# Leaving out the product of mean and inverse root in one batch's normalisation

## The chip, the cores and the metric

The kernel runs on one core of a Trainium2 chip. The core has five engines with a queue each: TensorE (PE, matmuls), VectorE (DVE), ScalarE (ACT), GpSimd (POOL) and SyncE (SP, which issues most DMAs). The metric is the device time of one execution in microseconds, as the median of several runs.

## The reference, cut to what matters

A windowed attention with sink columns feeds a gated MLP block. The change lies in the layer normalisation of the MLP's second half, `v`.

```python
x = attention(q, k, v, n_sink, window)          # 4 batches, 768 rows, 512 columns
h = gelu_tanh(x @ w_in)                         # 1024 columns
u, v = h[..., :512], h[..., 512:]
mu = mean(v, -1); var = mean((v - mu) ** 2, -1)
v_n = (v - mu) / sqrt(var + 1e-6) * g_ln
v_s = einsum('ts,bsd->btd', w_sg, v_n) + b_sg[None, :, None]
out = x + (u * v_s) @ w_out
```

## The kernel before, in words

Attention is done for 16 pairs of heads (numbers 0 to 15, four to a batch). The MLP block follows once for each of the four batches b = 0 to 3 and is woven into the attention of the next pairs. A batch's 768 rows are six tiles j = 0 to 5 of 128 rows.

Every step of the program is an operation with a name, such as `hv13` (batch 1, tile 3). The string `FIRST` lists all names in the order in which they are written out, and the string `TAKERS` says which engine takes a step that could go to several. `Planner.run` walks through `FIRST`; each engine gets its instructions in that order and runs them in order. Waits between engines are semaphores. So the order on each engine is written out by hand, and an operation that is removed moves nothing but what stands behind it on its own engine.

The steps of one batch that the prediction speaks of are these:

- `hv` b j: PE makes the tile's 512 columns of v (L751). `gelu_v` (ACT, L762) writes them to `v_all`.
- `bn` b j: DVE takes statistics and aggregates them (L773, L774). Mean and variance go to columns 0 and 1 of `mv`, a tile with three numbers for each of the six row tiles.
- `rstd` b 0 and `rstd` b 3: POOL adds 1e-6 to three variances (L818) and raises them to the power -0.5 (L820), for tiles 0 to 2 and for tiles 3 to 5.
- `shift` b 0 and `shift` b 3: DVE writes minus mean times inverse root to column 2 of `mv` (L826).
- `vn` b j: the normalised tile, in bfloat16. On DVE it is (v - mean) times inverse root in one instruction (L840), which reads columns 0 and 1. On ACT it is scale times v plus bias (L836), and the bias is column 2.
- `sp` b f m a and b: PE multiplies vn by the transposed `w_sg` (L864), tiles 0 to 2 in part a and tiles 3 to 5 in part b. `gate` and `gT` (DVE) follow, then `pj` (PE, the output projection).

`TAKERS` gives all six vn of batch 1 to DVE; batches 0, 2 and 3 give some of theirs to ACT. The vn of batch 1 stand in `FIRST` as vn10 vn11 vn12, then vn15, vn14, vn13. Around them POOL casts the pairs' rows to bfloat16 (L249: `cast_k`, `cast_q`, `cast_v`).

Of the kernel before, what the change touches and what calls it, by code (L numbers as in the profile page):

```python
# [49 lines left out]
class Planner:  # L50
# [15 lines left out]
    def add(self, *args, **kwargs):  # L66
        op = Op(*args, **kwargs)
        self.ops.append(op)
        return op
# [86 lines left out]
    "peek_DVE copied look"  # L156
)
TAKERS = (
    "zero_a0:ACT zero_a1:DVE zero_a2:DVE zero_a3:DVE low_a:DVE zero_b0:DVE zero_b1:DVE "
# [19 lines left out]
def kernel(  # L179
# [49 lines left out]
        vn=([128, NT, DF], BF16), gT=([128, KU, S], BF16), gv=([128, NH], BF16),  # L229
        o_sb=([128, DM], F32), st=([128, 6], F32))  # L230

    def tile_of(tag):
        shape, dtype = shapes[tag]
        return work.tile(shape, dtype, name=tag, tag=tag, bufs=R[tag].size)
# [6 lines left out]
    T = {}  # L241
    add = plan.add
# [10 lines left out]
    WARM = 8  # L253
    AHEAD = (0, 1)
    LAST = (2, 3)
    MARK = (B - 1, 3)
    LONG = ()
    BY_DMA = (11,12,13,14,15)
# [76 lines left out]
    def make_mask(m, at):  # L335
        for h in range(2):
# [6 lines left out]
                    rank=-2000)  # L343
    T["dark0"] = add("dark0", {"DVE": 450}, lambda _: make_dark0(), [T["dark"]], use=[dark],
                     rank=-1998)
    T["mask"] = add("mask", {"DVE": 600}, lambda _: make_mask(mask, 1), [T["dark"]],
                    use=[dark], rank=-300)
    T["mask0"] = add("mask0", {"DVE": 600}, lambda _: make_mask(mask0, 0), [T["dark0"]],
                     use=[dark], rank=-299)

    if LONG:
        T["spread"] = add("spread", {"POOL": 900}, lambda _: make_spread(), new=[spread],
                          rank=-378)
# [83 lines left out]
    def pos(n):  # L437
        return divmod(n, HP)
# [371 lines left out]
    def normalise(b, js, rank):  # L810
        mv = T["mv", b]
        lo, hi = js[0], js[-1] + 1
        if lo == 0:
            T["vn", b] = Buf(R["vn"])
        vn, v_all = T["vn", b], T["v_all", b]

        def root(_):
            nc.gpsimd.tensor_scalar(out=mv.tile[:, lo:hi, 1:2], in0=mv.tile[:, lo:hi, 1:2],  # L818
                                    scalar1=1e-6, scalar2=None, op0=ALU.add)
            nc.gpsimd.tensor_tensor(out=mv.tile[:, lo:hi, 1], in0=mv.tile[:, lo:hi, 1],  # L820
                                    in1=half[:, lo:hi], op=ALU.pow)

        r = add(f"rstd{b}{lo}", {"POOL": 1250}, root, [T["bn", b, j] for j in js], use=[mv],
                rank=rank)
        def shift(_):
            nc.vector.scalar_tensor_tensor(  # L826
                out=mv.tile[:, lo:hi, 2], in0=mv.tile[:, lo:hi, 0], scalar=-1.0,
                in1=mv.tile[:, lo:hi, 1], op0=ALU.mult, op1=ALU.mult)

        r = add(f"shift{b}{lo}", {"DVE": 160}, shift, [r], use=[mv], rank=rank)  # L830
        for j in js:
            def norm(e, j=j):
                if j == 0:
                    vn.tile = tile_of("vn")
                if e == "ACT":
                    nc.scalar.activation(out=vn.tile[:, j, :], in_=v_all.tile[:, j, :],  # L836
                                         func=AF.Identity, scale=mv.tile[:, j, 1:2],
                                         bias=mv.tile[:, j, 2:3])
                else:
                    nc.vector.tensor_scalar(  # L840
                        out=vn.tile[:, j, :], in0=v_all.tile[:, j, :],
                        scalar1=mv.tile[:, j, 0:1], scalar2=mv.tile[:, j, 1:2],
                        op0=ALU.subtract, op1=ALU.mult)
            T["vnorm", b, j] = add(
                f"vn{b}{j}", {"DVE": 700, "ACT": 800}, norm, [r] + ([T["vnorm", b, 0]] if j else []),
                new=[vn] if j == 0 else [], use=[v_all, mv] + ([vn] if j else []),
                rank=rank + 1)

# [41 lines left out]
    def project(b, t, rank, rooms):  # L890
# [3 lines left out]

        halves = [slice(0, DM)] if (b, t) != LAST else \
            [slice(0, DM // 2), slice(DM // 2, DM)]
# [115 lines left out]
    def turn_g(_):  # L1012
# [5 lines left out]
            rank=9000)  # L1018
# [39 lines left out]
    for n in range(NP):  # L1058
        r = 100 * n
        b, hp = pos(n)  # L1060
# [73 lines left out]

    held_o = T["o_sb", *MARK]

# [18 lines left out]
    for e in EARLY:  # L1155
        add("peek" if e == "SP" else f"peek_{e}", {e: 100 if e == "DVE" else 750}, peek, [a], rank=0)
    T["st", -1, 0] = add("copied", {"DVE": 150}, copied, [a, T["st", *MARK]], use=[held_o],
                         rank=0)
# [183 lines left out]
```

## Time and profile before

| | |
|---|---|
| median of 3 runs | 161.76 us (161.67 to 161.82) |
| the profiled execution's own time | 163.07 us |
| its span, first to last instruction | 161.1 us |
| mean granted clock of PE | 0.996 |
| instructions | 4001 |
| from HBM, to HBM | 24.81 MB, 6.29 MB |

The table says that the profile was taken of an execution 1.31 us above the median, with 1.94 us outside its span. A row of a timeline gives start, duration, engine, line, operation, the tiles written and read, their shapes and a count; in brackets stands how long the engine was idle before it, and what ended that.

### The profile page before, as it was taken

How to read it: one execution, taken by the hardware profiler on the slowest of the kernel's cores; microseconds unless marked ns; L12 is line 12 of the kernel's file. 1: busy time of each engine (PE TensorE's matmuls, PEld its weight loads, DVE VectorE, ACT ScalarE, POOL GpSimd, SP SyncE). 2: the span in 40 equal slices, each digit the busy share in tenths (PEclk: the TensorE clock that was granted, in tenths of full speed). 3: DMA queues.
4: the chain of work that ended last, by engine and by line, in shares of the span. 5: the costliest groups of instructions: out<-in, count | busy, mean ns of one | idle time of the engine just before them, and what ended most of it. 6: DMA issues, size and time to landing. Idle time of an engine off the chain costs nothing. (4 is left out here: it accounts for less than half of the span.)

```text
span 161.1 us, 4001 instructions
## 1 busy us (share of the span) xinstructions
PE 150.1 (93%) x1547; PEld 87.3 (54%) x1562; DVE 130.5 (81%) x283; ACT 107.5 (67%) x143; POOL 83.6 (52%) x126
## 2 busy tenths in 40 slices
PE   6789999998899999999989999999999999999980
PEld 2335665566656766546556555555556645555540
DVE  7555678695898989969999979868999969888980
ACT  6168878695989877988857778665997168811100
POOL 3465761228688789067975880865579602300000
PEclk9999999999999999999999999999999999999998
DMA  4999999998999986999988889999993340140163
GB/s 146 299 270 305 205 151 206 168 289 231 358 336 240 342 130 163 241 315 234 215 142 209 209 177 216 206 300 257 241 216 114 90 158 0 50 148 4 65 259 141
DMA packets 67877, 32.42 MB, mean 201 GB/s; under 512 B 56564, under 2 KB 64772, under 8 KB 67856
## 3 DMA queue, kind: packets, MB, share of 16 engines
q1 hardware_dynamic: 65328, 29.26, 69.5%
q0 software_dynamic: 2384, 2.75, 10.8%
q8 instruction: 13, 0.21, 0.6%
q10 hardware_dynamic: 144, 0.13, 0.2%
q14 instruction: 8, 0.07, 0.1%
HBM read 24.81 MB, written 6.29 MB: 193 GB/s over the span
## 5 line engine op out<-in xcount | busy, mean ns | idle before, releaser
L627 ACT ACTIVATE ex<-sc 128x1024 bf16<-128x1024 f32 x48 | 47.4, 1024 | 10.5 <-PE sc L610 10.4
L864 PE MATMUL vs<-wsgT,vn 128*128 128x384 bf16 x192 | 35.5, 326 | 1.6 <-DVE vn L840 1.0
L864 PEld LDWEIGHTS <-vn 128*128 128x128 bf16 x192 | 17.5, 98 | 13.2 <-issue 1.6
L793 PE MATMUL hu<-xT,w_in_sb 128*128 128x384 bf16 x128 | 23.4, 326 | 0.0
L801 ACT ACTIVATE uT<-hu 128x384 bf16<-128x384 f32 x32 | 14.9, 490 | 12.3 <-PE hu L793 12.1
L907 PE MATMUL o_ps<-w_out_sb,gT 128*128 128x512 bf16 (+1 forms) x91 | 22.6, 370 | 0.5
L751 PE MATMUL hv<-w_in_sb,xT 128*128 128x512 bf16 x94 | 22.4, 379 | 0.1
L875 DVE SCALAR_TENSOR_TENSOR vs<-vs,g_sb,b_bc 128x384 f32<-128x384 f32 x32 | 19.5, 619 | 2.6 <-PE vs L864 1.3
L773 DVE BATCH_NORM_STATS2 st<-v_all 128x6 f32<-128x512 f32 x24 | 16.3, 678 | 6.5 <-ACT v_all L762 6.5
L311 POOL TENSOR_SCALAR_AFFINE_SELECT ex<-ex 128x512 bf16<-128x512 bf16 (+1 forms) x23 | 15.4, 670 | 9.7 <-ACT ex L627 9.4
L610 PE MATMUL sc<-qT,kT 64*128 64x256 bf16 (+2 forms) x320 | 18.9, 249 | 0.9 <-ACT qT L247 0.5
L249 POOL CAST cast<-k_f 128x768 bf16<-128x768 f32 x16 | 13.4, 840 | 12.0 <-DMA k_f<-in_k_dram 9.4
L676 PEld LDWEIGHTS <-ex 128*128 128x128 bf16 x480 | 16.8, 97 | 4.0 <-issue 1.4
L695 DVE TENSOR_TENSOR x<-av,rcps 128x384 bf16<-128x384 f32 x32 | 17.5, 552 | 0.9
L883 DVE TENSOR_TENSOR gT<-vs,uT 128x384 bf16<-128x384 f32 x32 | 17.5, 555 | 0.9
L676 PE MATMUL av<-v_sb,ex 128*128 128x65 bf16 x352 | 18.0, 194 | 0.1
L249 POOL CAST cast<-q_f 128x768 bf16<-128x768 f32 x15 | 13.0, 869 | 9.7 <-DMA q_f<-in_q_dram 5.0
L918 DVE TENSOR_TENSOR o_sb<-o_ps,x 128x512 f32<-128x512 f32 (+1 forms) x25 | 16.2, 663 | 1.3 <-PE o_ps L907 1.2
L762 ACT ACTIVATE v_all<-hv 128x512 f32<-128x512 f32 x24 | 13.7, 598 | 5.2 <-PE hv L751 5.0
L793 PEld LDWEIGHTS <-w_in_sb 128*128 128x128 bf16 x128 | 12.3, 98 | 8.7 <-issue 0.2
L249 POOL CAST v_sb<-v_f 128x768 bf16<-128x768 f32 x16 | 13.9, 869 | 3.1 <-DMA v_f<-in_v_dram 3.1
L751 PEld LDWEIGHTS <-xT 128*128 128x128 bf16 x96 | 9.2, 98 | 10.5 <-DVE xT L249 0.6
(71 smaller groups left out, 194.2 us busy)
## 6 DMA issues: line engine op xcount, KB each, us to landing
k_f<-in_k_dram SPq DMA_DIRECT2D x16, 384.0 KB, 5.9
q_f<-in_q_dram SPq DMA_DIRECT2D x16, 384.0 KB, 5.2
v_f<-in_v_dram SPq DMA_DIRECT2D x16, 384.0 KB, 6.3
out_dram<-o_sb SPq DMA_DIRECT2D x23, 256.0 KB, 2.2
wsg<-in_moe_w_sg_dram POOLq DMA_DIRECT2D x2, 576.0 KB, 10.8
w_in_sb<-in_moe_w_in_dram POOLq DMA_DIRECT2D x2, 512.0 KB, 8.0
w_out_sb<-in_moe_w_out_dram POOLq DMA_DIRECT2D x1, 512.0 KB, 8.3
b_bc<-in_moe_b_sg_dram SPq DMA_DIRECT2D x1, 384.0 KB
```

What stands on the lines that cost most here:

```text
L249: eng[e].tensor_copy(dst, src)
L610: nc.tensor.matmul(sc.tile[row:row + keys, h, col:col + m], kT.tile[rows, k0:k0 + keys], qT.tile[rows, q0:q0 + m], start=not by_pe, stop=n ...
L627: nc.scalar.activation(out=ex.tile, in_=sc.tile, func=AF.Exp, scale=scale)
L676: nc.tensor.matmul(av.tile[:, m, h, :], ex.tile[:, h, col:col + 128], val, start=first, stop=(m == HT - 1 and h == 1 and at == len(steps) ...
L695: nc.vector.tensor_mul(x.tile[:, hp, HT * c:HT * (c + 1), :].rearrange("p i (h d) -> p i h d", h=2), av.tile[:, :, :, 0:64], rcp.to_broadc ...
L751: nc.tensor.matmul(ps.tile[:, 0:512], xT.tile[:, c, 128 * j:128 * (j + 1)], w_in_sb[:, c, DF:], start=(c == 0), stop=(c == KD - 1))
L773: nc.vector.bn_stats(out=st.tile, in_=v_all.tile[:, j, :])
L793: nc.tensor.matmul(ps.tile[:, 0:NH], w_in_sb[:, c, 128 * f:128 * (f + 1)], xT.tile[:, c, NH * m:NH * (m + 1)], start=(c == 0), stop=(c == ...
L864: nc.tensor.matmul(ps.tile[:, 0:NH], vn.tile[:, si, 128 * f:128 * (f + 1)], wsgT[:, si, cols], start=(si == 0), stop=(si == NT - 1))
L875: nc.vector.scalar_tensor_tensor(out=ps.tile[:, 0:NH], in0=ps.tile[:, 0:NH], scalar=g_sb[:, f:f + 1], in1=b_bc[:, cols], op0=ALU.mult, op1 ...
L883: nc.vector.tensor_mul(gT.tile[:, f, cols], ps.tile[:, 0:NH], uT.tile[:, f, cols])
L907: nc.tensor.matmul(ps.tile[:, 0:w], gT.tile[:, c, 128 * t:128 * (t + 1)], w_out_sb[:, c, cols], start=(c == 0), stop=(c == KU - 1))
```

## The change

The two operations `shift10` and `shift13` are taken out of `FIRST`, and for batch 1 `normalise` no longer makes them. The vn of these groups then follow `rstd` directly, and only DVE may take them. Column 2 of `mv` stays unwritten in batch 1, and nothing reads it there.

```diff
-    "gelu_u130 hu111 gelu_u101 gelu_u111 hu131 sc90 sc91 shift10 bn14 vn10 vn11 gelu_u131 exp91 "
-    "vn12 load_v11 load_k12 load_q12 rstd13 shift13 vn15 pv80 pv81 vn14 vn13 cast_q10 cast_k11 "
...
+    "gelu_u130 hu111 gelu_u101 gelu_u111 hu131 sc90 sc91 bn14 vn10 vn11 gelu_u131 exp91 vn12 "
+    "load_v11 load_k12 load_q12 rstd13 vn15 pv80 pv81 vn14 vn13 cast_q10 cast_k11 dma_k11 rcp80 "
...
     LAST = (2, 3)
+    NO_SHIFT = {(1, 0), (1, 3)}
     MARK = (B - 1, 3)
...
-        r = add(f"shift{b}{lo}", {"DVE": 160}, shift, [r], use=[mv], rank=rank)
+
+        if (b, lo) not in NO_SHIFT:
+            r = add(f"shift{b}{lo}", {"DVE": 160}, shift, [r], use=[mv], rank=rank)
...
-                f"vn{b}{j}", {"DVE": 700, "ACT": 800}, norm, [r] + ([T["vnorm", b, 0]] if j else []),
+                f"vn{b}{j}", {"DVE": 700} if (b, lo) in NO_SHIFT else {"DVE": 700, "ACT": 800}, norm, [r] + ([T["vnorm", b, 0]] if j else []),
```

On DVE, from the aggregate of `bn15` to the first reciprocal of pair 8 (`rcp80`), stood before:

```order
L774 BN_AGGR mv<-st 128x2 [waits DVE_49]
L826 SCALAR_TENSOR_TENSOR mv<-mv 128x3 [waits Pool_49]
L773 BN_STATS st<-v_all 128x6 [waits Activation_49]
L774 BN_AGGR mv<-st 128x2 [waits DVE_49]
L840 TENSOR_SCALAR vn<-v_all,mv 128x512 x3
L826 SCALAR_TENSOR_TENSOR mv<-mv 128x3 [waits DVE_49,Pool_49]
L840 TENSOR_SCALAR vn<-v_all,mv 128x512 x3
L689 RECIPROCAL rcps<-av 128x6 [waits PE_49]
```

The rows of L826 are `shift10` and `shift13`, the rows of L840 the six vn. In the same place on DVE stands now (line numbers are higher by two from there on):

```order
L774 BN_AGGR mv<-st 128x2 [waits DVE_49]
L773 BN_STATS st<-v_all 128x6 [waits Activation_49]
L774 BN_AGGR mv<-st 128x2 [waits DVE_49]
L842 TENSOR_SCALAR vn<-v_all,mv 128x512 [waits Pool_49]
L842 TENSOR_SCALAR vn<-v_all,mv 128x512 x2
L842 TENSOR_SCALAR vn<-v_all,mv 128x512 [waits Pool_49]
L842 TENSOR_SCALAR vn<-v_all,mv 128x512 [waits DVE_49]
L842 TENSOR_SCALAR vn<-v_all,mv 128x512
L689 RECIPROCAL rcps<-av 128x6 [waits PE_49]
```

Two rows are gone, and `bn14` (the statistics and the aggregate) stands directly behind `bn15`. The waits for POOL that the two products carried are now on `vn10` and `vn15`; the wait for an earlier instruction of DVE itself, which `shift13` carried, is on `vn14`. The rows of PE, ACT, POOL and SP up to the end of the computation are the same in number and order.

More of the change, by code (lines that the diff above doesn't have):

```diff
@@ L122 @@
     "gelu_v14 turn_q9 cols_q9 hu101 turn_k10 cols_k10 hu121 gelu_u121 hu120 gelu_u120 hu130 "
[33 rows of a table removed]
-    "peek_DVE copied look"
[33 rows of a table added]
 )
```

62 rows, old and new, of the table FIRST are left out of this document.

## The prediction

> **What bounds the kernel now.** I read the page's busy shares first, then the table of waits, then the timelines of the engines around the one wait that the table left. TensorE (PE) is busy nearly all the time:
>
> ```profile
> PE 150.1 (93%) x1547; PEld 87.3 (54%) x1562; DVE 130.5 (81%) x283; ACT 107.5 (67%) x143; POOL 83.6 (52%) x126
> ```
>
> The waits of PE in the window from 42 to 153 us, that is from the middle of the first batch's block to the last projections, are one row (waiter, who ended it, total us, times, longest):
>
> ```profile
> PE vs L864 <- DVE vn L840: 1.0, 1, 1.0
> ```
>
> So for 110 us PE runs without a pause except one, and that one is ended by a normalised row (vn) from VectorE. The timeline of PE puts it at 81 us, in the second batch:
>
> ```profile
> 79.61 0.65 PE L864 MATMUL vs<-wsgT,vn 128*128 128x384 bf16 x3
> 81.26 0.66 PE L864 MATMUL vs<-wsgT,vn 128*128 128x384 bf16 x3 [0.99 <-DVE vn L840]
> 81.75 0.50 PE L550 MATMUL cps<-iden,cast 128*128 128x128 bf16 x6
> ```
>
> The first three matmuls of batch 1's spatial product (sp100a) start at 79.61; the next three (sp100b) need rows 3 to 5 of vn and start at 81.26. Three matmuls of this kind take 81.75 - 81.26 = 0.49 us from start to start, so sp100b could have begun at 79.61 + 0.49 = 80.10. PE loses 81.26 - 80.10 = **1.16 us** there. Since PE never waits again before 153 us, what it wins here it can keep.
>
> What made vn late is seen on VectorE (DVE; start, duration):
>
> ```profile
> 74.05 0.18 DVE L774 BATCH_NORM_AGGREGATE mv<-st 128x2 f32<-128x6 f32 x1
> 74.21 0.78 DVE L826 SCALAR_TENSOR_TENSOR mv<-mv 128x3 f32<-128x3 f32 x1
> 74.91 0.68 DVE L773 BATCH_NORM_STATS2 st<-v_all 128x6 f32<-128x512 f32 x1
> 75.62 0.18 DVE L774 BATCH_NORM_AGGREGATE mv<-st 128x2 f32<-128x6 f32 x1
> 75.72 1.43 DVE L840 TENSOR_SCALAR vn<-v_all,mv 128x512 bf16<-128x512 f32 x3
> 77.47 0.77 DVE L826 SCALAR_TENSOR_TENSOR mv<-mv 128x3 f32<-128x3 f32 x1 [0.32 <-POOL mv L820]
> 78.16 3.04 DVE L840 TENSOR_SCALAR vn<-v_all,mv 128x512 bf16<-128x512 f32 x3
> 81.12 0.18 DVE L689 RECIPROCAL rcps<-av 128x6 f32<-128x6 f32 x1
> ```
>
> and beside it on GpSimd (POOL):
>
> ```profile
> 74.15 0.82 POOL L249 CAST v_sb<-v_f 128x768 bf16<-128x768 f32 x1
> 75.89 0.43 POOL L818 TENSOR_SCALAR mv<-mv 128x3 f32<-128x3 f32 x1 [0.93 <-DVE mv L774]
> 76.41 1.03 POOL L820 TENSOR_TENSOR mv<-mv,half 128x3 f32<-128x3 f32 x1
> 77.40 0.82 POOL L249 CAST cast<-q_f 128x768 bf16<-128x768 f32 x1
> 78.17 0.82 POOL L249 CAST cast<-k_f 128x768 bf16<-128x768 f32 x1
> 78.94 1.02 POOL L249 CAST v_sb<-v_f 128x768 bf16<-128x768 f32 x1
> 79.91 1.01 POOL L249 CAST cast<-q_f 128x768 bf16<-128x768 f32 x1
> 81.29 0.65 POOL L311 TENSOR_SCALAR_AFFINE_SELECT ex<-ex 128x512 bf16<-128x512 bf16 x1 [0.37 <-ACT ex L627]
> ```
>
> The two removed instructions are the rows of L826 at 74.21 and 77.47. They work on three numbers per partition, yet take 0.78 and 0.77 us. All eight of their kind (count: min/median/max in ns):
>
> ```profile
> L826 DVE SCALAR_TENSOR_TENSOR mv<-mv x8: 131/461/775, 33.8 to 139.6; 128x3 f32<-128x3 f32 x8
> ```
>
> The two in batch 1 start 0.06 and 0.07 us behind a cast on POOL and end 0.02 us after it (74.99 beside 74.97, 78.24 beside 78.22). So the work is 0.13 us, and the rest is held by the cast. The same is seen on vn: three alone take 1.43 us, three beside casts 3.04, and the casts beside them go from 0.82 to 1.02. There DVE and POOL take turns, one vn and one cast in (81.12 - 78.16) / 3 = 0.99 us.
>
> **The change part by part.** *shift10, at 74.21.* Next on DVE is the last statistics instruction (bn14). Its input is the third row here on ScalarE (ACT):
>
> ```profile
> 73.56 0.60 ACT L762 ACTIVATE v_all<-hv 128x512 f32<-128x512 f32 x1 [0.27 <-PE hv L751]
> ...
> 80.19 1.02 ACT L627 ACTIVATE ex<-sc 128x1024 bf16<-128x1024 f32 x1
> 82.29 0.80 ACT L247 COPY qT<-cps 128x768 bf16<-128x768 bf16 x1 [1.08 <-PE cps L550]
> ```
>
> It is there at 73.56 + 0.60 = 74.16, so bn14 can start at about 74.20 in place of 74.91. Would the cast hold it as it held shift10? A statistics row and a cast that lay over each other earlier:
>
> ```profile
> 70.41 0.66 DVE L773 BATCH_NORM_STATS2 st<-v_all 128x6 f32<-128x512 f32 x1
> ```
>
> ```profile
> 70.88 0.83 POOL L249 CAST cast<-k_f 128x768 bf16<-128x768 f32 x1 [1.34 <-DMA k_f<-in_k_dram]
> ```
>
> Both kept their length, so statistics are not held. The removal is worth 74.91 - 74.20 = 0.71 us. With it move vn10 to vn12 (75.72 to 75.01) and, since POOL's chain for rows 3 to 5 waits for the last statistics (the row at 75.89), that chain too: its power ends at 76.41 + 1.03 - 0.71 = 76.73, and the cast of q that follows starts at 77.40 - 0.71 = 76.69.
>
> *shift13, at 77.47.* Now vn15 waits for the power itself, and may start at 76.73 + 0.03 = 76.76. It lands 0.07 us behind a cast, just as shift13 did, so this wait does not go away: it passes to vn15. What goes is one whole turn. Before, the order at the port was q cast, shift13, k cast, vn15, v cast, vn14, q cast, vn13; now it is q cast, vn15, k cast, vn14, v cast, vn13. Before, the three vn took from 78.17 (start of the first cast beside them) to 81.20; now the first cast beside them starts at 76.69, which gives 76.69 + 3.03 = 79.72, or 76.76 + 3.04 = 79.80 counted from vn15. I take 79.80. vn14 has a wait of its own for an earlier DVE instruction, which shift13 carried before: it costs nothing if that is long done (the statistics are), at most 0.11 us, since an aggregate, which waits for the statistics in front of it, starts 0.03 us after their end (75.59, 75.62) where a row without such a wait starts 0.08 us before it (78.24, 78.16). 79.91 then.
>
> *PE.* sp100b needs vn13 0.06 us ahead (81.20, then 81.26), so by 80.04. Either end meets this with 0.1 us or more to spare, and the gain is PE's whole 1.16 us. Were the second removal worth nothing, vn13 would end at 81.20 - 0.71 = 80.49 and PE would gain 0.71; it cannot gain more than 1.16 here, since PE is then never idle.
>
> *What the pause covered.* Behind sp100b PE turns q's columns (81.75), and ACT copies them at 82.29 after 1.08 us of idle. The exponential in front of that copy, 80.19 to 81.21, hangs on PE's earlier scores and does not move. 1.16 us earlier the copy would start at 81.13, and ACT is free at 81.21 at the latest. The cover is used up to within 0.08 us, and that is the most that a slip here costs. The number of instructions and their order on PE, ACT, POOL and SP do not change, and no DMA is moved past another.
>
> *Sum.* The profiled execution took 163.07 us (its span 161.1 and 1.94 around it): 163.07 - 1.16 = 161.91. It stood 1.31 above the median of the three runs, 161.76; I carry the gain over unchanged: **160.60 us**.
>
> *Turns against a rule.* The turn of 0.99 us is a measured one, less than a cast and a vn alone one behind the other. The Trainium skill, GPSIMD Engine Reference, section 8 (Key points), says that GpSimd shares its memory interfaces with VectorE and collides with vector instructions that read two tensors from SBUF or run in a two-port mode; Advanced Engine Details and Errata, section VectorE Performance Modes, says that the two block each other. On who is held (shift, vn) and who is not (statistics) the trace agrees; taken strictly, the rule allows no overlap, which is the first rival below with 161.15 us, and I follow the 0.99 of the rows.
>
> **The rivals.** *Full turns (161.15).* If a vn and a cast could not overlap at all, a turn would be 0.82 + 1.43 / 3 = 1.30 us, vn13 would end at 76.69 + 3 x 1.30 = 80.59, and PE would gain 81.20 - 80.59 = 0.61. Against it stands the 0.99 of the same three vn before.
>
> *One turn lost (161.35).* vn15 could lose the port to two casts in place of one, since it now comes to it right behind a power and a cast instead of behind shift13. vn13 then ends 0.99 later, 80.79, sp100b starts at 80.85, and PE gains 0.41. For it: it has not been seen which of the two wins when both arrive. Against it: at 78.16 and later they took strict turns.
>
> *No turns (161.76, no change).* POOL could keep the port through its run of four casts, at 0.77 us from start to start (77.40, 78.17): until 76.69 + 3.08 = 79.77, then three vn in 1.43: 81.20, as before. Against it: the casts at 78.94 and 79.91 were themselves lengthened by vn. That the change does not do what it says, because a shift's own work is only 0.13 us and the hold passes on whole, comes out here too.
>
> *A load decides in batch 2 (slower).* The same products remain in batch 2, where one ran free:
>
> ```profile
> 104.11 0.84 POOL L249 CAST cast<-k_f 128x768 bf16<-128x768 f32 x1 [0.46 <-DMA k_f<-in_k_dram]
> ...
> 105.36 0.89 POOL L820 TENSOR_TENSOR mv<-mv,half 128x3 f32<-128x3 f32 x1
> 106.20 0.82 POOL L249 CAST v_sb<-v_f 128x768 bf16<-128x768 f32 x1
> ```
>
> ```profile
> 107.29 0.13 DVE L826 SCALAR_TENSOR_TENSOR mv<-mv 128x3 f32<-128x3 f32 x1
> ...
> 111.65 0.99 DVE L840 TENSOR_SCALAR vn<-v_all,mv 128x512 bf16<-128x512 f32 x2
> ```
>
> ```profile
> 112.95 0.97 PE L864 MATMUL vs<-wsgT,vn 128*128 128x384 bf16 x5
> ```
>
> shift20 came 0.27 us after the cast of v ended (107.02). DVE comes 1.16 earlier now, at 106.13; POOL's chain begins with a cast that waits for the load of k of pair 14. If that load does not move, shift20 is held until 107.04, 0.78 late. The last vn ends at 112.64, its matmul, fourth from 112.95, starts at 113.44: 0.8 us of slack, so a load that stays where it was costs about nothing. Each tenth by which it lands later than before costs a tenth. From 1.16 + 0.32 = 1.5 us late the kernel is slower, at 2 us late it takes 161.76 - 1.16 + 2.0 = 162.6. Loads of this kind take 5.9 us at the median:
>
> ```profile
> k_f<-in_k_dram SPq DMA_DIRECT2D x16, 384.0 KB, 5.9
> ```
>
> so 2 us is not out of the question, but nothing in the change delays them: the issues stand behind work that comes earlier.
>
> **How the numbers follow.** A difference of 0.2%, 0.32 us, is about what a measurement of this kernel can tell from no change. The forecast, 160.45 to 160.75 with the 0.15 us by which the three runs differ, gets 0.69; more than that 0.03; full turns 0.05; one turn lost, or the second removal worth nothing (161.05 to 161.35), 0.09; no change 0.08; slower 0.06. Faster is 0.69 + 0.03 + 0.05 + 0.09 = 0.86. The range from 160.4 to 161.4 holds the forecast and the two rivals with part of the gain, 0.83.
>
> **What the profile after would show.** Six rows of the product in place of eight; bn14 at about 74.20; three vn from 75.01; POOL's power ending at 76.73; three more vn, each about a microsecond, ending near 79.8; sp100b at 80.10 with no wait of PE; then PE's rows all 1.16 earlier to the end. Wrong would be: bn14 held beside the cast; a vn of batch 1 over 1.2 us; a wait of PE at 80 to 81; or a new wait of PE behind 85 us, which would name what took the gain.

## The result, and the profile after

The changed kernel took 161.0 us at the median of 14 runs, the kernel before 161.8 at the median of 14 beside it: ratio 0.9939, 95% interval 0.9913 to 0.9964. The forecast, 160.60 against 161.76, is a ratio of 0.9928 and lies inside. On the scale of the forecast the measured ratio is 161.76 x 0.9939 = 160.77 us. All ratios are of the fast executions alone; the profile of before is of one that counts as slow, but the part of it that is compared below is no longer than in the repeats (71.47 us beside 71.71 and 71.62). The profiled execution of the changed kernel took 161.97 us (span 160.0, mean granted clock 0.984), 1.10 less than the profiled one of before; the forecast for it was 161.91. That these two agree to 0.06 us is luck: the profiled repeats of the changed kernel took 160.30 and 160.70.

The engines of the page of after:

```profile
PE 151.5 (95%) x1562; PEld 88.0 (55%) x1562; DVE 128.5 (80%) x281; ACT 107.5 (67%) x143; POOL 83.7 (52%) x126
```

DVE has two instructions fewer and 2.0 us less of busy time. The waits of PE from 42 to 153 us, in the same table as before the change:

```profile
PE sc L610 <- DMA qT<-cast: 0.2, 1, 0.2
```

The wait for vn is gone, and a small one for a transposed q is new. On PE's timeline of after, the changed place, the new wait, and the row with which the last projections begin:

```profile
79.55 1.14 PE L866 MATMUL vs<-wsgT,vn 128*128 128x384 bf16 x6
80.52 0.50 PE L550 MATMUL cps<-iden,cast 128*128 128x128 bf16 x6
...
119.60 0.39 PE L610 MATMUL sc<-qT,kT 64*128 64x256 bf16 x4 [0.22 <-DMA qT<-cast]
...
150.14 5.35 PE L909 MATMUL o_ps<-w_out_sb,gT 128*128 128x512 bf16 x28
```

sp100a and sp100b are one row of six matmuls now, with no pause between them. The changed place begins 0.06 us earlier than before (79.55 against 79.61) for reasons that lie ahead of it, so 0.06 is to be taken off when the two traces are laid side by side. DVE and POOL of after, at the place:

```profile
73.98 0.18 DVE L774 BATCH_NORM_AGGREGATE mv<-st 128x2 f32<-128x6 f32 x1
74.12 0.69 DVE L773 BATCH_NORM_STATS2 st<-v_all 128x6 f32<-128x512 f32 x1
74.85 0.18 DVE L774 BATCH_NORM_AGGREGATE mv<-st 128x2 f32<-128x6 f32 x1
74.95 1.43 DVE L842 TENSOR_SCALAR vn<-v_all,mv 128x512 bf16<-128x512 f32 x3
76.70 2.96 DVE L842 TENSOR_SCALAR vn<-v_all,mv 128x512 bf16<-128x512 f32 x3 [0.33 <-POOL mv L820]
79.58 0.18 DVE L689 RECIPROCAL rcps<-av 128x6 f32<-128x6 f32 x1
```

```profile
74.09 0.82 POOL L248 CAST v_sb<-v_f 128x768 bf16<-128x768 f32 x1
75.12 0.43 POOL L818 TENSOR_SCALAR mv<-mv 128x3 f32<-128x3 f32 x1 [0.21 <-DVE mv L774]
75.64 1.03 POOL L820 TENSOR_TENSOR mv<-mv,half 128x3 f32<-128x3 f32 x1
76.63 0.82 POOL L248 CAST cast<-q_f 128x768 bf16<-128x768 f32 x1
77.40 1.02 POOL L248 CAST cast<-k_f 128x768 bf16<-128x768 f32 x1
78.36 1.01 POOL L248 CAST v_sb<-v_f 128x768 bf16<-128x768 f32 x1
79.33 1.01 POOL L248 CAST cast<-q_f 128x768 bf16<-128x768 f32 x1
```

The statistics at 74.12 lie fully beside the cast at 74.09 and kept their 0.69 us. The vn behind POOL's power (76.70) start 0.07 us behind a cast and take turns with the three that follow, which grow from 0.82 to 1.02 and 1.01. The last vn ends at 76.70 + 2.96 = 79.66. And ACT, whose idle time ahead of the copy was used up:

```profile
80.12 1.02 ACT L627 ACTIVATE ex<-sc 128x1024 bf16<-128x1024 f32 x1
81.06 0.80 ACT L246 COPY qT<-cps 128x768 bf16<-128x768 bf16 x1
```

The copy starts 1.23 us earlier than before (82.29), directly behind the exponential.

**How the traces were compared.** A profiled execution differs from the next one of the same kernel by more than the change is worth, and most of that arises ahead of the change: the first spatial product of batch 0 began at 41.59 in the profile of before and at 39.58 in that of a repeat of the changed kernel. PE in the one and in the other:

```profile
41.59 1.62 PE L864 MATMUL vs<-wsgT,vn 128*128 128x384 bf16 x9 [0.57 <-ACT uT L801]
```

```profile
39.58 1.62 PE L866 MATMUL vs<-wsgT,vn 128*128 128x384 bf16 x9 [0.31 <-ACT uT L801]
```

So I measure, in each trace, from the start of sp100a (79.61 before) to the row of the last projections. That row of before:

```profile
151.08 5.35 PE L907 MATMUL o_ps<-w_out_sb,gT 128*128 128x512 bf16 x28
```

That is 151.08 - 79.61 = 71.47 us before, and 150.14 - 79.55 = 70.59 after: 0.88 less. The pause of 1.16 is gone whole, and 0.28 went back later, all of it at the new wait at 119.60: counted from sp100a, PE's rows stand where they do in the second trace of the changed kernel (further down) up to there, and 0.28 later from there on. Three traces of each kernel follow with the repeats.

### The profile page after: what moved, and what is told of

It is laid out like the page before. It is cut to its first block, busy times and chain, and to the rows that moved or that the text cites. A ratio compares the mean times of both kernels' runs of the same rounds, so it can differ in the third digit from the quotient of the medians.

```text
span 160.0 us, 4013 instructions
## 1 busy us (share of the span) xinstructions
PE 151.5 (95%) x1562; PEld 88.0 (55%) x1562; DVE 128.5 (80%) x281; ACT 107.5 (67%) x143; POOL 83.7 (52%) x126
## 5 line engine op out<-in xcount | busy, mean ns | idle before, releaser
L866 PE MATMUL vs<-wsgT,vn 128*128 128x384 bf16 x192 | 35.4, 326 | 0.2 <-ACT uT L801 0.2
L866 PEld LDWEIGHTS <-vn 128*128 128x128 bf16 x192 | 17.6, 98 | 11.6 <-issue 1.1
L909 PE MATMUL o_ps<-w_out_sb,gT 128*128 128x512 bf16 (+1 forms) x100 | 23.1, 371 | 0.0
L248 POOL CAST cast<-k_f 128x768 bf16<-128x768 f32 x16 | 13.9, 866 | 12.5 <-DMA k_f<-in_k_dram 9.8
L610 PE MATMUL sc<-qT,kT 64*128 64x256 bf16 (+2 forms) x320 | 19.4, 253 | 0.7 <-ACT qT L246 0.5
L311 POOL TENSOR_SCALAR_AFFINE_SELECT ex<-ex 128x512 bf16<-128x512 bf16 (+1 forms) x23 | 15.1, 657 | 6.7 <-ACT ex L627 6.6
L762 ACT ACTIVATE v_all<-hv 128x512 f32<-128x512 f32 x24 | 13.7, 598 | 5.2 <-PE hv L751 5.0
```

What stands on the lines that cost most here:

```text
L248: eng[e].tensor_copy(dst, src)
L610: nc.tensor.matmul(sc.tile[row:row + keys, h, col:col + m], kT.tile[rows, k0:k0 + keys], qT.tile[rows, q0:q0 + m], start=not by_pe, stop=n ...
L866: nc.tensor.matmul(ps.tile[:, 0:NH], vn.tile[:, si, 128 * f:128 * (f + 1)], wsgT[:, si, cols], start=(si == 0), stop=(si == NT - 1))
L909: nc.tensor.matmul(ps.tile[:, 0:w], gT.tile[:, c, 128 * t:128 * (t + 1)], w_out_sb[:, c, cols], start=(c == 0), stop=(c == KU - 1))
```

## The experiments

The theory is that of the prediction: a cast on POOL holds the products, each hold delays the vn, and with both gone vn13 is in time. Its rivals are that the products' place on DVE or the waits they carry are the cost, whoever runs beside them; and, for what is gained, that something later takes it back. An edit shifts the lines below it, so the same statement stands under neighbouring numbers: L840 to L842 is vn on DVE, L864 to L866 its matmul.

### The kernel before again, twice

> The kernel before, unchanged, timed against itself and profiled once more. Theory (the pause of TensorE is fixed by the order on VectorE and GpSimd): shift13 0.77 us, three vn beside casts about 3.0 us, a pause of 1.0 to 1.16 us whatever the start of the execution did; the ratio shows what two sets of runs of one kernel differ by, 0.997 to 1.003. Rival (the pause hangs on when a load lands, since shift10 was held 0.78 us in one execution and 0.44 in another): shift10 between 0.13 and 0.78 us and a pause that moves with it, 0.5 to 1.16 us, so that the median gain is smaller than the one of the first profile.

> The kernel before once more, one look, for the same question: is shift10 held for 0.77 us and the pause 1.16 us in this execution too (theory), or is one of them smaller (rival)?

Nothing is edited. PE in the first of the two:

```profile
78.28 0.65 PE L864 MATMUL vs<-wsgT,vn 128*128 128x384 bf16 x3
80.15 0.66 PE L864 MATMUL vs<-wsgT,vn 128*128 128x384 bf16 x3 [1.21 <-DVE vn L840]
...
149.99 5.35 PE L907 MATMUL o_ps<-w_out_sb,gT 128*128 128x512 bf16 x28
```

The pause is there in all three executions: sp100b starts late by 1.16 us in the profile of before, by 80.15 - 78.28 - 0.49 = 1.38 here, by 1.30 in the second repeat (78.94, 80.73). Both products took 0.77 or 0.78 us each time, as the theory said, but 1.38 and 1.30 lie above its 1.0 to 1.16. DVE in the first repeat shows why:

```profile
72.72 0.18 DVE L774 BATCH_NORM_AGGREGATE mv<-st 128x2 f32<-128x6 f32 x1
73.11 0.77 DVE L826 SCALAR_TENSOR_TENSOR mv<-mv 128x3 f32<-128x3 f32 x1 [0.21 <-POOL mv L820]
73.80 0.68 DVE L773 BATCH_NORM_STATS2 st<-v_all 128x6 f32<-128x512 f32 x1
```

shift10 also waits for POOL's first power. It starts 0.39 us after the aggregate in front of it here and 0.32 in the second repeat, but 0.16 in the profile of before (74.05, 74.21): 0.23 and 0.16 more, and the pause is 0.22 and 0.14 longer. In all three sp100a starts 5.56 or 5.57 us after that aggregate, so the date on PE is fixed, and the pause grows with the time from the aggregate to bn14: 0.86, 1.08 and 1.02 us. POOL's chain in front of the power begins with a cast that waits for a load of k (idle 1.33 us before 69.77 here), so the rival is right in that the pause moves with a load, though not through the length of shift10.

The time of the first repeat against its own kernel was 161.58 to 161.36, ratio 0.9996 (0.9958 to 1.0035), which shows what a comparison of equals gives; the second repeat is a single execution, at 162.32.

### The changed kernel again, twice

> The changed kernel once more, beside the next two on the same chip. All theories: no pause of TensorE at 80 us, ratio to the kernel before 0.990 to 0.997. If the new wait of TensorE near 119.6 us (for qT of pair 15) is part of the kernel, it is there again with 0.1 to 0.5 us; if it was chance of that execution, it is gone.

> The changed kernel once more, timed in five rounds. Theory (no pause left; the wait for qT of pair 15 in the first profile was chance of that execution): no wait of TensorE listed from 64 to 153 us; from the start of sp100a to the last projection 75.4 us, against 76.6 to 76.8 in the three executions of the kernel before; ratio 0.992 to 0.997. Rival (the wait for qT is part of the kernel): it is there in about one look of two, with 0.2 to 0.4 us.

Nothing is edited. PE in the first of the two:

```profile
78.11 1.14 PE L866 MATMUL vs<-wsgT,vn 128*128 128x384 bf16 x6
...
148.43 5.35 PE L909 MATMUL o_ps<-w_out_sb,gT 128*128 128x512 bf16 x28
```

Neither repeat has any row in the table of waits of PE, from 42 us to the last projections: the wait at 119.60 belongs to the one execution. The times were 160.73 to 161.48, ratio 0.9967 (0.9938 to 0.9997), and 160.39 to 161.91, ratio 0.9916 (0.9876 to 0.9956). By the traces, from sp100a to the row of the last projections (the expectation counted on to the start of the last projection in it, some 5.1 us more):

| | first | second | third | mean |
|---|---|---|---|---|
| before, us | 71.47 | 71.71 | 71.62 | 71.60 |
| its pause, us | 1.16 | 1.38 | 1.30 | 1.28 |
| before less the pause, us | 70.31 | 70.33 | 70.32 | 70.32 |
| after, us | 70.59 | 70.32 | 70.52 | 70.48 |

Without its pause every trace of before comes to the same 70.32, and the second trace of after is just that. So the pause is the whole difference, and the other two traces of after gave 0.28 and 0.20 back. The 0.20 of the third is lost in batch 2. Its DVE and PE there:

```profile
104.84 0.34 DVE L826 SCALAR_TENSOR_TENSOR mv<-mv 128x3 f32<-128x3 f32 x1
```

```profile
109.64 0.42 PE L676 MATMUL av<-v_sb,ex 128*128 128x65 bf16 x8
```

The first row is shift20, beside a cast of POOL that ended at 105.16, 0.02 before it; in the second trace it took 0.15. Counted from sp100a, shift23, ACT's vn and uT behind it and then this row of PE all start 0.20 us later than in the second trace.

The change is worth 71.60 - 70.48 = **1.12 us** there, a ratio of 160.64 / 161.76 = 0.9931 on the median of before. The three measured ratios lie on both sides of it, 0.9941 at the mean; two of their intervals hold it, and the third ends at 0.9938, a gain of 1.0 us.

### Only the first product left out

```diff
-    "gelu_u130 hu111 gelu_u101 gelu_u111 hu131 sc90 sc91 shift10 bn14 vn10 vn11 gelu_u131 exp91 "
+    "gelu_u130 hu111 gelu_u101 gelu_u111 hu131 sc90 sc91 bn14 vn10 vn11 gelu_u131 exp91 "
...
-        r = add(f"shift{b}{lo}", {"DVE": 160}, shift, [r], use=[mv], rank=rank)
+        if (b, lo) != (1, 0):
+            r = add(f"shift{b}{lo}", {"DVE": 160}, shift, [r], use=[mv], rank=rank)
```

> Only the first product (shift10) is left out; shift13 stays. Theory (each product takes its own slot on VectorE and both slots reach TensorE): the last statistics start at about 74.2 instead of 74.9, shift13 is still held by the cast of q (0.77 us) but comes 0.71 us earlier, vn13 ends near 80.5 instead of 81.2, TensorE's pause at the spatial product falls from 1.16 us to about 0.45 (0.99 to about 0.3 in the table of waits), and the time falls by 0.7 us. Rival A (the wait for GpSimd's power sets the chain and the first product is hidden behind it): power and vn13 end where they did, no change in time. Rival B (only the 0.13 us of work counts): vn13 0.1 us earlier, no change that can be measured.

DVE and PE of this kernel:

```profile
75.07 0.77 DVE L826 SCALAR_TENSOR_TENSOR mv<-mv 128x3 f32<-128x3 f32 x1 [0.32 <-POOL mv L820]
75.75 3.04 DVE L841 TENSOR_SCALAR vn<-v_all,mv 128x512 bf16<-128x512 f32 x3
```

```profile
77.92 0.65 PE L865 MATMUL vs<-wsgT,vn 128*128 128x384 bf16 x3
78.85 0.66 PE L865 MATMUL vs<-wsgT,vn 128*128 128x384 bf16 x3 [0.28 <-DVE vn L841]
```

The pause is 78.85 - 77.92 - 0.49 = 0.44 us in place of 1.16: the first removal is worth 0.72 beside the profile of before, and 0.71 was worked out; beside the mean pause of the three traces, 1.28, it is worth 0.84, since the wait for POOL's first power goes with it. The second product is held as before. The time, 160.9 to 161.2, ratio 0.9971 (0.9935 to 1.0006), agrees and alone would not prove a gain.

### Only the second product left out, twice

```diff
-    "vn12 load_v11 load_k12 load_q12 rstd13 shift13 vn15 pv80 pv81 vn14 vn13 cast_q10 cast_k11 "
+    "vn12 load_v11 load_k12 load_q12 rstd13 vn15 pv80 pv81 vn14 vn13 cast_q10 cast_k11 "
...
-        r = add(f"shift{b}{lo}", {"DVE": 160}, shift, [r], use=[mv], rank=rank)
+        if (b, lo) != (1, 3):
+            r = add(f"shift{b}{lo}", {"DVE": 160}, shift, [r], use=[mv], rank=rank)
```

> Only the second product (shift13) is left out; shift10 stays and is held as before. Theory (the wait behind the cast passes to vn15, and one turn with the casts is won): vn15 starts at about 77.5 and takes about 1.03 us, vn13 ends near 80.5, TensorE's pause falls from 1.16 to about 0.47 us, the time falls by 0.7 us. Rival A (the hold passes on whole, so that the second removal is worth only its 0.13 us of work): vn13 ends at 81.1, the pause stays above 1.0 us. Rival B (the second removal alone clears the pause): vn13 ends before 80.1, no pause.

The first execution had no pause at all. PE, then the first product on DVE, then the cast beside it on POOL:

```profile
79.15 1.14 PE L865 MATMUL vs<-wsgT,vn 128*128 128x384 bf16 x6
```

```profile
73.69 0.44 DVE L826 SCALAR_TENSOR_TENSOR mv<-mv 128x3 f32<-128x3 f32 x1
```

```profile
73.29 0.82 POOL L249 CAST v_sb<-v_f 128x768 bf16<-128x768 f32 x1
```

shift10 came 0.40 us after the start of the cast instead of 0.06, and was held for 0.44 instead of 0.77. It ended at 74.13, once more 0.02 us after the cast (74.11). So the hold is what is left of the cast, and it depends on when the cast happened to start. The sizes fit: from the aggregate (73.59) to bn14 (74.05) are 0.46 us, 0.40 less than the 0.86 in the profile of before, and about 0.4 was the pause that should have been left. The missing pause was not expected, and I ran the kernel once more, asking whether the pause of 0.4 us comes back with a cast that starts beside the product.

> Only the second product left out, one more look. In the first look shift10 was held 0.44 us instead of 0.78 and the pause was gone, which no theory had expected. Theory (the hold of shift10 hangs on where the cast beside it lies, and the two effects add): if shift10 is held about 0.77 again, the pause is 1.16 - 0.77 = about 0.4 us; if it is held less, the pause is smaller by as much. Rival (the second removal alone clears the pause): no pause, whatever shift10 took.

```profile
74.69 0.78 DVE L826 SCALAR_TENSOR_TENSOR mv<-mv 128x3 f32<-128x3 f32 x1
...
77.95 2.96 DVE L841 TENSOR_SCALAR vn<-v_all,mv 128x512 bf16<-128x512 f32 x3 [0.33 <-POOL mv L820]
```

```profile
80.08 0.65 PE L865 MATMUL vs<-wsgT,vn 128*128 128x384 bf16 x3
80.96 0.66 PE L865 MATMUL vs<-wsgT,vn 128*128 128x384 bf16 x3 [0.22 <-DVE vn L841]
```

It took 0.78 again, and the pause is 80.96 - 80.08 - 0.49 = 0.39 us. From the aggregate to bn14 are 0.86 us here as in the profile of before, so the two pauses can be compared: the second removal is worth 1.16 - 0.39 = 0.77 us. The times were 161.1 to 161.2, ratio 0.9986 (0.9959 to 1.0012), which does not show a gain, and a single execution at 162.71. The two halves add up to 0.72 + 0.77 = 1.49, more than the pause of 1.16: with both gone, vn13 is about 0.3 us early, and the change has that much to spare.

### Both products kept, but written out later

```diff
-    "gelu_u130 hu111 gelu_u101 gelu_u111 hu131 sc90 sc91 shift10 bn14 vn10 vn11 gelu_u131 exp91 "
-    "vn12 load_v11 load_k12 load_q12 rstd13 shift13 vn15 pv80 pv81 vn14 vn13 cast_q10 cast_k11 "
+    "gelu_u130 hu111 gelu_u101 gelu_u111 hu131 sc90 sc91 bn14 vn10 vn11 gelu_u131 exp91 "
+    "vn12 load_v11 load_k12 load_q12 rstd13 vn15 pv80 pv81 vn14 vn13 cast_q10 cast_k11 "
...
-    "pj10 exp111 band111 load_k13 band110 pv100 pv101 store11 xT8 xT9 rcp101 x101 o10 store10 "
+    "pj10 exp111 band111 load_k13 band110 pv100 pv101 store11 xT8 xT9 shift10 shift13 rcp101 x101 o10 store10 "
...
-        r = add(f"shift{b}{lo}", {"DVE": 160}, shift, [r], use=[mv], rank=rank)
+        made = add(f"shift{b}{lo}", {"DVE": 160}, shift, [r], use=[mv], rank=rank)
+        if b != 1:
+            r = made
```

> Both products are still computed for batch 1, but the six vn no longer come after them: they stand together some 14 us later on VectorE, ahead of a reciprocal that waits for TensorE. Theory (it is the place that costs, not the instruction): the same as the changed kernel, vn13 ends near 79.7, no pause of TensorE at the spatial product, the two products cost nothing where they stand now, time 0.8 to 1.16 us below the kernel before. Rival (the number of instructions or of semaphore waits counts): some of the gain is missing, or a new wait of TensorE shows behind 90 us.

This is the changed kernel with the two products put back behind the vn, 11 us later. PE and DVE:

```profile
78.19 1.14 PE L866 MATMUL vs<-wsgT,vn 128*128 128x384 bf16 x6
```

```profile
89.59 0.67 DVE L826 SCALAR_TENSOR_TENSOR mv<-mv 128x3 f32<-128x3 f32 x2
```

The pause is gone although the products are made. So it was their place, in front of the vn and beside the casts, that cost time, and not the number of instructions. At the new place the two together took 0.67 us: the first ended at 90.18, and beside it POOL had not a cast but a mask select (L311, 89.32 to 90.17). So they are not free there, as the expectation had it: from sp100a to the last projections it took 148.84 - 78.19 = 70.65, which is 0.33 more than the 70.32 of an undisturbed trace, lost on PE between 91.0 and 91.6 us. Timed: 160.7 to 161.2, ratio 0.9978 (0.9940 to 1.0016), which alone would not show the gain.

### The casts held back instead

```diff
-    "vn12 load_v11 load_k12 load_q12 rstd13 shift13 vn15 pv80 pv81 vn14 vn13 cast_q10 cast_k11 "
+    "vn12 load_v11 load_k12 load_q12 rstd13 shift13 vn15 pv80 pv81 vn14 vn13 hold_casts cast_q10 cast_k11 "
...
+    def hold_casts(_):
+        nc.gpsimd.tensor_copy(apart, T["vn", 1].tile[0:1, 3, 0:1])
...
+        if b == 1:
+            add("hold_casts", {"POOL": 200}, hold_casts, [T["vnorm", b, 3]], use=[T["vn", b]])
```

> The kernel before with both products, but GpSimd reads one element of vn13 ahead of the cast of q of pair 10 (one more 1x1 copy on GpSimd), so that its four casts run after vn13 instead of beside shift13 and the last three vn. Theory (the casts hold shift13 and vn): shift13 takes at most 0.16 us, the three vn 1.43 us together instead of 3.04, vn13 ends near 79.0, TensorE has no pause at the spatial product, although nothing was left out; the time falls by up to 1.16 us, less what the casts, now 1.4 us later, give back behind it. Rival (the length is the instructions' own, such as the landing of the power's result): shift13 still 0.77 us and each vn above 1 us, the pause stays.

Both products stay at their place; a copy of one number on POOL waits for vn13, so that no cast lies beside shift13 and the vn behind it. DVE and POOL:

```profile
77.71 0.17 DVE L826 SCALAR_TENSOR_TENSOR mv<-mv 128x3 f32<-128x3 f32 x1 [0.32 <-POOL mv L820]
77.79 1.45 DVE L840 TENSOR_SCALAR vn<-v_all,mv 128x512 bf16<-128x512 f32 x3
```

```profile
79.32 0.18 POOL L1040 CAST apart<-vn 1x1 f32<-1x1 bf16 x1 [1.64 <-DVE vn L840]
79.44 0.82 POOL L249 CAST cast<-q_f 128x768 bf16<-128x768 f32 x1
```

shift13 falls from 0.77 to 0.17 us and the three vn from 3.04 to 1.45, with not an instruction of theirs touched. That separates the casts from the products' place on DVE and from the waits they carry. In the same execution shift10, whose cast stayed where it was, still took 0.77. PE has no pause at the place, yet the kernel is slower, where a gain of up to 1.16 us was expected: 165.57 to 161.2, ratio 1.0187 (1.0088 to 1.0286). PE's timeline shows why:

```profile
79.63 1.14 PE L864 MATMUL vs<-wsgT,vn 128*128 128x384 bf16 x6
...
93.26 0.61 PE L610 MATMUL sc<-qT,kT 64*128 64x256 bf16 x4 [2.08 <-DMA qT<-cast]
```

The casts start 2 us later, and what hangs on them, the transposes of pair 12 in SP's queue, lands late: from 64 to 153 us PE has one wait, of 2.1 us for `qT`. PE falls 3.8 us behind (153.73 - 79.63 = 74.10 to the last projections, beside 70.32). The other 1.7 us goes with the clock: behind the wait the granted clock of PE was 0.50 from 93.2 to 96 us and 0.73 in the next microsecond, where the profile of before has 1.00. Why it fell is open, since it stayed at 1.00 behind a wait of 2.00 us in another trace (the last section). So the 3.8 us are not all the price of late casts. Four casts cannot be held back at this place; two products can be left out.

### Can the wait for pair 15 be taken away?

Two edits of the changed kernel aim at the wait of 119.60, one by earlier loads, one by casting q before v:

```diff
-    "load_v14 dma_k14 hu220 gelu_u220 bn22 rstd20 band120 bn24 hv23 gelu_v23 bn23 shift20 bn25 "
+    "load_v14 load_k15 load_q15 dma_k14 hu220 gelu_u220 bn22 rstd20 band120 bn24 hv23 gelu_v23 bn23 shift20 bn25 "
...
-    "o13 load_k15 load_q15 pj15 o15 vn21 vn25 cast_q14 dma_q14 gelu_u211 vn23 sc130 hu221 hu231 "
+    "o13 pj15 o15 vn21 vn25 cast_q14 dma_q14 gelu_u211 vn23 sc130 hu221 hu231 "
```

```diff
-    "sc140 exp140 gate210 gT210 sp211a sp211b gate211 cast_v14 gT211 cast_q15 store13 dma_k15 "
+    "sc140 exp140 gate210 gT210 sp211a sp211b gate211 gT211 cast_q15 store13 dma_k15 cast_v14 "
```

> The changed kernel with the loads of k and q of pair 15 issued ahead of the transposing DMA of k of pair 14 instead of behind it. Theory (what was given back is a load that did not move with TensorE): cast of k of pair 15 starts at 110 to 111 instead of 112.7, the wait for qT of pair 15 is gone, time 0.2 to 0.3 us below the changed kernel, the full 1.16 below the kernel before. Rival (the DMA queue is full there and only the order of what waits changes): the wait stays, or moves to the scores of pair 14 near 115.6, whose kT comes later; time equal or up to 1 us longer than the changed kernel.

> The changed kernel with GpSimd's cast of q of pair 15 ahead of the cast of v of pair 14. Theory (the load of q, landed at 114.0, sets the cast): the cast starts at 114.0 instead of 114.2, the wait for qT of pair 15 falls by at most 0.2 us, time within 0.2 us of the changed kernel. Rival (GpSimd's order sets it): the wait is gone and 0.3 us are won. Other rival: the products of pair 14 wait for the cast of v, TensorE pauses before 119 us, and the time rises by some tenths.

In the profile after, the cast of k of pair 15 waited for its load. POOL of after, then of the kernel with earlier loads:

```profile
112.66 0.83 POOL L248 CAST cast<-k_f 128x768 bf16<-128x768 f32 x1 [3.37 <-DMA k_f<-in_k_dram]
```

```profile
110.53 0.83 POOL L248 CAST cast<-k_f 128x768 bf16<-128x768 f32 x1 [1.01 <-DMA k_f<-in_k_dram]
```

Counted from sp100a (79.55, and 79.79 with earlier loads) the cast starts 30.74 us behind in place of 33.11, and neither kernel shows a wait of PE behind the place of the change; to the last projections they take 70.50 and 70.31 us. In the two repeats of the changed kernel that cast stands at 32.20 and 32.51 without any edit, and there was no wait either. The times of the two edited kernels, 160.77 and 160.61 beside 160.73 of the changed kernel in the same comparison, are equal to it within the intervals (against before: 0.9965, 0.9937 to 0.9993, and 0.9949, 0.9912 to 0.9986). Since the wait is also absent from two of the three traces of the changed kernel, there is little to gain here, and whether either edit removes it for good is not decided.

## Why the prediction was right, point by point

- **PE's one pause sets the time.** Right. Three traces of before have it, three of after do not, and less their pause those of before agree to 0.02 us. The time between fixed points fell by 1.12 us where 1.16 was forecast, but the two sizes agree partly by luck. The pause is 1.16, 1.38 and 1.30: its mean, 1.28, was the term to use, and 0.28, 0 and 0.20 is lost later, 0.16 at the mean. That PE keeps what it wins, and that its rows come 1.16 earlier to the end, held in one trace of three; in the profile after they come 1.16 earlier, counted from sp100a, up to 119.60, and 0.88 from there on. The wait there is one of the prediction's own signs of being wrong, a new wait behind 85 us, at a size of 0.28.
- **shift10 worth 0.71 us.** Right for the trace it was read from: 0.72 by itself. bn14 starts at 74.12 + 0.06 = 74.18 on the clock of before (74.20 forecast), vn10 at 75.01 (75.01), and the power ends at 76.67 + 0.06 = 76.73 (76.73). The statistics were not held. Their input is the row of L762 at 73.56, the first in its fence and not the third. What the prediction left out is that shift10 also waits for the first power, which makes it dearer in the other two traces of before (from the aggregate to bn14 1.08 and 1.02 us, in place of 0.86).
- **shift13 worth one turn.** Right in kind, 0.08 us too small. Of the two ways of counting in the prediction, from the start of the first cast (79.72) and from vn15 (79.80), I took the second; the last vn ended at 79.66 + 0.06 = 79.72. The three turns run from the cast, and vn15's 0.07 us behind it is part of them. So the removal is worth 80.49 - 79.72 = 0.77, as the kernel without it alone showed, and not 0.69. The wait on vn14 cost nothing.
- **The cover on ACT.** Right: the copy at 81.06 had no idle time ahead of it, and PE did not wait for it.
- **Full turns, one turn lost, no turns.** All three fell: (79.58 - 76.70) / 3 = 0.96 us a turn, and strict turns from the first vn on. A turn is less than 0.82 + 0.48 = 1.30, a cast and a vn alone. The Trainium skill, Advanced Engine Details and Errata, section VectorE Performance Modes, says that GpSimd's instructions and VectorE's in two-port modes block each other. The trace agrees in that vn and casts lengthen each other (a vn from about 0.5 to 1.03 or 1.04 us, casts from 0.82 to 1.02), but a turn of 0.96 in place of 1.30 means that they also overlap by a quarter.
- **A load decides in batch 2.** It fell as a slower kernel, but it came in small. shift20 ran in 0.13 us in the profile after. In the second repeat the first cast of POOL's chain (102.26) waited 1.12 us for its load where it waited 0.79 in the first, shift20 was held to 0.34, and PE lost 0.20 us there. The prediction's 0.8 us of slack was read at the last vn and its matmul; by the rows that start later, the way over ACT's uT has none.
- **The level.** The forecast carried the gain from one profiled execution to the median of three runs, and that held, but nothing secured it: the first part of the kernel ends up to 2.5 us apart in like executions (39.58 to 42.06 for the first product of batch 0), by a cause that I did not look into. That spread is large enough to account for ratios from 0.9916 to 0.9967, but this was not tested, and the two repeats ran on different chips. 160.77 us lies inside the range of 160.4 to 161.4 and 0.02 above the narrow one, 160.45 to 160.75. The 0.2% that the prediction took for what a measurement can tell was too fine: a kernel against itself gave an interval of 0.4% to either side.

## What to carry to other kernels

A tiny instruction can cost as much as a large one beside it: look for short rows whose duration varies and see whether they end with an instruction on another engine. What such a row is worth is the wait that it ends in, not its length: here each of two was worth 0.7 to 0.9 us, both together 1.1 to 1.3, since the pause was no longer. Moving the row behind the urgent work brings most of this (all but 0.33 us here), and where its result isn't read, leaving it out is better still. Holding back the other engine was the dear way here, since its own readers then waited. A pause is best read from several executions: here it changed by 0.22 us with the end of one instruction on POOL.

## What the runs showed of the hardware that was not expected

- The hold is the rest of the cast: a 128x3 product took 0.13 to 0.17 us with no cast beside it, 0.44 behind a cast that was 0.40 old, 0.77 behind one just begun, and ended 0.01 to 0.03 us after the cast wherever a cast held it. A mask select of POOL (128x512, bfloat16) held it in the same way (90.18 beside 90.17).
- POOL is held as well: its power of 128x3 took 0.89 us with no vn beside it (72.43 in the first execution without the second product) and 1.03 beside vn, casts 0.82 and 1.02.
- Once there were no turns at all. In the profile of the kernel with earlier loads, far ahead of its edit, DVE and POOL:

```profile
43.21 3.65 DVE L638 TENSOR_TENSOR ex<-ex,mask 128x1024 bf16<-128x1024 bf16 x1
```

```profile
43.73 0.84 POOL L248 CAST cast<-k_f 128x768 bf16<-128x768 f32 x1
44.51 0.66 POOL L311 TENSOR_SCALAR_AFFINE_SELECT ex<-ex 128x512 bf16<-128x512 bf16 x1
45.11 0.42 POOL L316 TENSOR_SCALAR_AFFINE_SELECT ex<-ex 128x256 bf16<-128x256 bf16 x1
45.49 0.82 POOL L248 CAST cast<-q_f 128x768 bf16<-128x768 f32 x1
```

The multiplication, 0.68 to 1.43 us at this place in the other twelve traces, ended at 46.86, 0.55 after the last of four instructions of POOL, none of which was lengthened by more than 0.02; PE waited 2.00 us for what stood behind it, and its granted clock stayed at 1.00. Why vn takes turns and this one did not stays open.
